# Block-sparse attention with a gated feed-forward layer: a second PSUM bank for the gate projections of two units, pad columns zeroed on VectorE, and a planner told longer load latencies

## The chip, the cores and the metric

The kernel runs on one core of a Trainium2 chip. A core has five engines that run side by side, each through its own list of instructions in order: TensorE (PE, matrix products into PSUM), VectorE (DVE), ScalarE (ACT), GpSimd (POOL) and SyncE (SP, which here only issues DMAs). They wait for each other through semaphores. The time is the device time of one execution in microseconds; lower is better.

## The reference, cut to what matters

First an attention over 4 batches, 8 heads, 768 positions and 64 columns per head, with a mask over blocks of 32 positions:

```python
scores = scale * np.matmul(q, k.transpose(0, 1, 3, 2))
mask = np.abs(blk_i - blk_j) <= window
mask = mask | (blk_i == 0) | (blk_j == 0) | (blk_i == n_blocks - 1) | (blk_j == n_blocks - 1)
for qb in range(n_blocks):
    for kb in sampled_blocks[qb]:
        mask[qb * block:(qb + 1) * block, kb * block:(kb + 1) * block] = True
scores = np.where(mask, scores, -1000000000.0)
scores = scores - np.max(scores, axis=-1, keepdims=True)
attn = np.exp(scores)
attn = attn / (np.sum(attn, axis=-1, keepdims=True) + 1e-09)
return np.matmul(attn, v).astype(np.float32)
```

Its output, laid out as 3072 tokens of 512 columns, is the input of the second part, with d_ff of 1536:

```python
rms = np.sqrt(np.mean(x * x, axis=-1, keepdims=True) + 1e-06)
xn = x / rms * rms_g
g = xn @ w_gate
silu = g * (1.0 / (1.0 + np.exp(-g)))
val = xn @ w_val
return (silu * val @ w_out).astype(np.float32)
```

## The kernel before, in words

All 768 x 768 scores are computed. The mask is part of the product: each row of q and k has 64 columns of data, and 24 more columns (one per key block) that add 0 or a large negative number, so 88 in all. These rows stand in two buffers `aug`, padded to 128 columns.

**Groups.** A group g is a pair of heads of one batch; there are 16, four per batch. For the four groups of batch 0, TensorE transposes the rows (`tp`, line 257) into PSUM, and an engine copies them into a slot of `XA` (`ev`, evacuation; `evx`, lines 260 to 262). For later groups the rows are loaded (`ld`), cast into `aug` (`fill`) and v into `vaug` (`pv`), and one transposing DMA, issued by SP, brings a whole group into `XA` (`turn`, line 243). It transposes all 128 columns, so the 40 pad columns must have been zeroed once (`zp`, line 247). `XA` has five slots. The q rows of columns 3 to 5 of batch 0 come by one load `q2`, and are cast by `fq` g 3.

**Units.** A unit u is a stretch of tokens of one batch: units 0, 1 and 2 are 128 tokens each, units 3 to 9 are 384 each (`UNITS`, lines 51 and 52). For each unit and each of the four pairs of heads come the scores (`qk`, line 275, in steps of 768 score columns that fill two PSUM banks), `exp` on ScalarE (line 290), the attention-value product `av` (line 304, bank 7, for units 0 to 2 also bank 6), and on VectorE the division `xo` (lines 315 and 316). When the four pairs are done come the square sums `sq`, the root `rsq` on GpSimd (line 333) and the scaling `xq` (line 340), then xn, the transposed input of the second part. For units below `NPET` (4 here) TensorE transposes xq (`tr`, line 351) and ScalarE or VectorE copies it (`cp`, line 359); for the others a transposing DMA does both (`xt`, line 366).

**Second part.** For each step f of a unit's d_ff: the gate projection `g` (line 378, bank 4), tanh of it on ScalarE (`th`, line 387), `uu` on VectorE (line 393), the value projection `v` (line 378, bank 5), and `hp` on VectorE (line 404). Last the output product `y` (line 417, bank 6), its copy `yo` and the store. `uu` gives the gate bank back and `hp` the value bank. Weights arrive in four chunks of w_gate and w_val (`wi` 0 to 3) and two of w_out, issued by GpSimd; chunks 2 and 3 are issued behind the roots of units 0 and 1. On SP a tiny DMA (`gate_sync`) waits for a chunk before the loads of groups 4 to 7.

**The order.** It is not written out by hand. A planner in the kernel (lines 689 to 753) holds a list of operations with the engines that may do each and a time for it, what it depends on, a priority, and what it takes and gives back (PSUM banks, buffers). It runs through a clock of its own, picks the operation that can start first and emits its instructions at once, on an engine of its choice where there are several. So a changed time, choice or bank can change the order on every engine from there on. On TensorE it also puts in dummy matmuls (`idle`) where it expects a gap within the first 24 us.

Behind a load, the planner counts 1.9 us (`LAT["DMA"]`) before the data is there, 8.0 for the loads of later batches:

```python
    end[o["key"]] = fin + (
        3.7 if o["key"] == ("q2",) else 8.0 if o["key"][0] == "ld" and o["key"][1] >= NP else 4.0 if o["key"][0] == "turn"
        else LAT[e])
```

Of the kernel before, what the change touches and what calls it, by code (L numbers as in the profile page):

```python
# [17 lines left out]
def kernel(  # L18
# [12 lines left out]
    nc = tc.nc  # L31
    SIMOUT = None
    P = 128
# [6 lines left out]
    NP = H // 2  # L40
# [3 lines left out]
    KQ = D + NB  # L44
    NSLOT, NAUG, NRAW, NOPEN = 5, 2, 3, 2
    AHEAD, HURRY, HURU = 0.8, ("av", "xo", "sq", "rsq", "xq", "tr", "cp"), 0
    NSTARV = 3
    AH = {"uu": 0.3, "hp": 0.3}
    WARM = (11, 10, 2)
    HD = NC * D // 2  # L50
# [3 lines left out]
    HG = [(b, c // 3) for b, c, n in UNITS]  # L54
# [16 lines left out]
    aug = [const.tile([P, 2, 2, NC, P], BF16, name=f"aug{i}") for i in range(NAUG)]  # L71
# [92 lines left out]
    for t in aug:  # L164
# [8 lines left out]
        op=ALU.is_equal)  # L173
# [24 lines left out]
    wg = const.tile([P, DM // P, DFF], BF16, name="wg")  # L198
# [45 lines left out]
            out=X[g % NSLOT].rearrange("p i e (c t) -> p (i e c) t", t=P),  # L244
            in_=aug[g % NAUG].rearrange("p i e c r -> p (i e c r)"))

    def zero_pad():
        for t in aug:
            nc.gpsimd.memset(t[:, :, :, :, KQ:P], 0.0)

    def tpx(g, i, es, lo, hi, bk):
        n = hi - lo
# [177 lines left out]
        dst = out[b * S:(b + 1) * S, :].rearrange("(p c) f -> p c f", c=NC)  # L430
        nc.sync.dma_start(out=dst[:, c0 + t, h * n:(h + 1) * n], in_=o)

    NPT, NXN, NHP, NPET = 3, 3, 2, 4
    pools = {n: [0.0] * c for n, c in (
        ("pt", NPT), ("hp", NHP), ("xo", 2), ("xq", 2), ("xn", NXN), ("raw", NRAW), ("va0", 1),
        ("va1", 1), ("th", 2), ("uu", 3))}
# [11 lines left out]
    def op(key, engs, deps, prio, fn, acq=(), rel=(), at=0.0):  # L448
        o = dict(key=key, engs=engs, deps=deps, prio=prio, fn=fn, acq=acq, rel=rel, at=at,
                 n=len(ops))  # L450
        ops.append(o)
        made[key] = o
# [56 lines left out]
    for g in range(NP):  # L509
        a_ = g % NAUG  # L510
        rr = [("raw", g)]
        if g:
            op(("fk", g), {"DVE": 0.57, "POOL": 0.84}, [("l", g, 0)], (-1, g, 0),
               lambda e, p, g=g: fillk(g, e), [(f"aK{a_}", g)], rr)
        for n_, (es, lo, hi) in enumerate(QP[g == 0]):
            dep = ("q2",) if lo == 3 else ("l", 0, 1, n_) if g == 0 else ("l", g, 1)
            pri = (-1, g, 1) if lo == 0 else (2.5, g, lo)
            fe = {"DVE": 0.09 + 0.085 * (hi - lo), "POOL": 0.1 + 0.13 * (hi - lo)}
            op(("fq", g, lo), {"ACT": 0.2} if g == 0 and lo == 0 else fe, [dep], pri,
               lambda e, p, a=(g, lo, hi): fillq(*a, e), [(f"a{'QR'[lo == 3]}{a_}", (g, lo == 3))],  # L520
               rr if lo < 3 else [("hp", ("q2",))])
        for i in range(2):
            for n_, (es, lo, hi) in enumerate((KP, QP)[i][g == 0]):
                m_ = len(es) * (hi - lo)
                if i == 0:
                    pri = (-1, g, 0.5 + 0.1 * n_ + (g == 0 and lo == 3))
                else:
                    pri = (-1, g, 1) if lo == 0 else (2.5, g, lo)
                res = f"aK{a_}" if i == 0 else f"a{'QR'[lo == 3]}{a_}"
                key = ("tp", g, i, es[0], lo)  # L530
                op(key, {"PE": m_ * 0.056}, [("fq", g, lo)] if i else [("fk", g)] if g else [],
                   pri, lambda e, p, a=(g, i, es, lo, hi): tpx(*a, p),
                   [(TP1[:1] if i and lo == 3 else TP1, key), (f"X{g}", g)],
                   [(res, g)] if i == 0 else [(res, (g, lo == 3))])
                de = {"DVE": 0.07 + m_ * P / 1560.0}
                ac = {"ACT": 0.15 + m_ * P / 1200.0}
                if g == 0 and i == 0:
                    de = (de, ac, {**de, **ac})[n_]
                elif i and lo == 3 or g == 0 and lo == 0:
                    de.update(ac)  # L540
                op(("ev",) + key[1:], de, [key], pri,
                   lambda e, p, a=(g, i, es, lo, hi): evx(*a, e), [], [(None, key)])
        op(("pv", g), {"DVE": 0.57, "POOL": 1.0}, [("l", g, 2)], (0, g, 2),
           lambda e, p, g=g: pad_v(g, e), [("va0", 0)], rr)
# [2 lines left out]
            pools[f"a{r_}{a_}"] = [0.0]  # L547
    held["aK0", 0] = "aK0"
    pools["aK0"] = []
    op(("zp",), {"POOL": 1.8}, [], (9,), lambda e, p: zero_pad(), at=24.0)  # L550
    for g in range(NP, B * NP):
        b, pr = divmod(g, NP)
        gate = {NP: 2, NP + 1: 3, NP + 2: 4, NP + 3: 5}.get(g)
        for i in range(3):
            def ld(e, p, g=g, i=i, gate=gate):
                if gate is not None and i == 0:
                    gate_sync(gate)
                load(g, i)
            op(("ld", g, i), {"DMA": 1.1}, [("w", gate)] if gate is not None and i == 0 else [],
               (1,), ld, [("raw", g)] if i == 0 else [])  # L560
            if i < 2:
                op(("fill", g, i), {"DVE": 0.57}, [("ld", g, i), ("zp",)] + [
                    ("tp", g_, i_, 0, 3 * i_) for g_ in (2, 3) for i_ in range(2)],
                   (4, g, i), lambda e, p, g=g, i=i: fill(g, i, e), [(f"aug{g % NAUG}", (g, False))])
            else:
                op(("pv", g), {"DVE": 0.57}, [("ld", g, 2), ("fill", g, 0), ("fill", g, 1)],
                   (4, g, 2), lambda e, p, g=g: pad_v(g, e), [(f"va{b % 2}", b)], [("raw", g)])
        op(("turn", g), {"DMA": 4.6}, [("fill", g, 0), ("fill", g, 1)], (-1, g),
           lambda e, p, g=g: turn(g), [(f"X{g % NSLOT}", g)], [(f"aug{g % NAUG}", (g, False))])
# [11 lines left out]
    for u, (b, c0, nt) in enumerate(UNITS):  # L581
        w, last = nt * P, c0 + nt == NC
        ng = NC // KT[nt]
        for pr in range(NP):
            g0 = b * NP + pr
            pk = pr // 2 if nt == 1 else pr
            for g in range(ng):
# [10 lines left out]
               lambda e, p, a=(u, pr): av(*a, p), [([(7,)] + [(6,)] * (u < 3), ("o", u, pr)), ("xo", u)],  # L598
               ([("pt", (u, pk))] if nt > 1 or pr % 2 else []) + ([(f"va{b % 2}", b)] if last and pr == NP - 1 else []))
            op(("xo", u, pr), {"DVE": 0.4 + w / 960.0}, [("av", u, pr)], (0, u, pr),  # L600
               lambda e, p, a=(u, pr): xo(*a), [], [(None, ("o", u, pr))])
# [18 lines left out]
        for f in range(NF // fg):  # L620
            n_ = fg * w
            op(("g", u, f), {"PE": fg * NP * mm(w)}, [("cp", u), ("w", w_of[f])], (4, u, f, 1),
               lambda e, p, a=(u, f): proj(*a, wg, "gp", p), [([(4,)], ("g", u, f)), ("hp", HG[u])])
            op(("th", u, f), {"ACT": 0.12 + n_ / 1200.0}, [("g", u, f)], (2, u, f),
               lambda e, p, a=(u, f): th(*a), [("th", (u, f))])
            op(("uu", u, f), {"DVE": 0.155 + n_ / 960.0}, [("th", u, f)], (2, u, f),
               lambda e, p, a=(u, f): uu(*a), [("uu", (u, f))],
               [(None, ("g", u, f)), ("th", (u, f))])
            op(("v", u, f), {"PE": fg * NP * mm(w)}, [("g", u, f)], (4, u, f, 0),
               lambda e, p, a=(u, f): proj(*a, wv, "vp", p), [([(5,)], ("v", u, f))],  # L630
               [("xn", u)] if f == NF // fg - 1 else [])
            op(("hp", u, f), {"DVE": 0.155 + n_ / 960.0}, [("uu", u, f), ("v", u, f)], (3, u, f),
               lambda e, p, a=(u, f): hp(*a), [],
               [(None, ("v", u, f)), ("uu", (u, f))])
# [54 lines left out]
    while ready:  # L689
# [27 lines left out]
        for names, key, nme in got:  # L717
# [9 lines left out]
        fin = t1 + o["engs"][e]  # L727
        free[e] = fin
        end[o["key"]] = fin + (
            3.7 if o["key"] == ("q2",) else 8.0 if o["key"][0] == "ld" and o["key"][1] >= NP else 4.0 if o["key"][0] == "turn"  # L730
            else LAT[e])
        if o["key"][0] in ("qk", "tr"):
            nqk -= 1
# [52 lines left out]
```

The softmax here doesn't subtract the row's maximum and nothing guards it: scores larger than these inputs give would overflow.

## Time and profile before

| | before |
|---|---|
| median of 7 runs (lowest to highest) | 312.06 us (311.75 to 315.37) |
| the profiled execution's own time | 312.06 us |
| its span, first to last instruction | 310.3 us |
| busy: TensorE, VectorE, ScalarE, GpSimd | 302.5, 191.4, 207.1, 24.3 us |
| granted TensorE clock | 1.000 |
| DMA: bytes, mean rate over the span | 42.42 MB, 137 GB/s |

Times are microseconds from the span's start. Matmuls overlap, so a group's duration is a little longer than the distance to the next group's start, and a short gap is seen in the starts more surely than in the row of waits. L and a number is a line of the kernel; the copies of many operations share line 113, and are told apart by their tiles.

### The profile page before, as it was taken

How to read it: one execution, taken by the hardware profiler on the slowest of the kernel's cores; microseconds unless marked ns; L12 is line 12 of the kernel's file. 1: busy time of each engine (PE TensorE's matmuls, PEld its weight loads, DVE VectorE, ACT ScalarE, POOL GpSimd, SP SyncE). 2: the span in 40 equal slices, each digit the busy share in tenths (PEclk: the TensorE clock that was granted, in tenths of full speed). 3: DMA queues.
4: the chain of work that ended last, by engine and by line, in shares of the span. 5: the costliest groups of instructions: out<-in, count | busy, mean ns of one | idle time of the engine just before them, and what ended most of it. 6: DMA issues, size and time to landing. Idle time of an engine off the chain costs nothing.

```text
span 310.3 us, 7395 instructions
## 1 busy us (share of the span) xinstructions
PE 302.5 (97%) x3063; PEld 200.7 (65%) x3063; DVE 191.4 (62%) x423; ACT 207.1 (67%) x325; POOL 24.3 (8%) x42
## 2 busy tenths in 40 slices
PE   8899999999999999999999999999999999999995
PEld 7898888766666656666666666666666545556543
DVE  5779655785668878766654844674489607727500
ACT  5988988688877877878777787878743133323221
POOL 3457200010000001001000100010001000000000
PEclk9999999999999999999999999999999999999999
DMA  6999999999999899931894030011000041010022
GB/s 210 315 233 195 195 268 221 215 307 282 228 306 196 227 214 323 235 122 36 159 159 75 34 87 2 34 38 49 2 34 3 17 127 45 0 70 0 0 105 101
DMA packets 70661, 42.42 MB, mean 137 GB/s; under 512 B 48356, under 2 KB 67556, under 8 KB 70628
## 3 DMA queue, kind: packets, MB, share of 16 engines
q1 hardware_dynamic: 64800, 37.23, 48.8%
q0 software_dynamic: 5792, 4.72, 9.7%
q8 instruction: 24, 0.39, 0.5%
q14 instruction: 9, 0.07, 0.1%
q10 hardware_dynamic: 36, 0.00, 0.0%
HBM read 28.57 MB, written 6.29 MB: 112 GB/s over the span
## 4 chain that ended last, share of the span: by engine, by line
PE 91%; DMA 3%; ACT 3%; DVE 2%; issue 1%; ACTq 0%; DVEq 0%; SPq 0%
PE PS L378 40%; PE PS L417 20%; PE PS L275 18%; PE PS L304 11%; ACT pt L290 2%; DMA qkv<-in_q_dram 2%; DMA xn<-xq 1%; PE PS L129 1%; PE PS L257 1%; DVE XA L113 1%; PE PS L351 0%; ACT th L387 0%; DVE uu L393 0%; DVE xo L316 0%; ACT XA L109 0%
## 5 line engine op out<-in xcount | busy, mean ns | idle before, releaser
L290 ACT ACTIVATE pt<-PS 128x768 bf16<-128x768 f32 x192 | 145.4, 812 | 35.2 <-PE PS L275 33.8
L393 DVE SCALAR_TENSOR_TENSOR uu<-th,PS 128x384 bf16<-128x384 bf16 x96 | 53.2, 554 | 62.3 <-ACT th L387 60.3
L275 PE MATMUL PS<-XA 88*128 88x384 bf16 (+1 forms) x480 | 81.4, 294 | 0.9 <-ACT pt L290 0.8
L378 PE MATMUL PS<-xn,wg 128*128 128x384 bf16 (+1 forms) x480 | 75.4, 294 | 1.1 <-DMA xn<-xq 0.7
L378 PE MATMUL PS<-xn,wv 128*128 128x384 bf16 (+1 forms) x480 | 75.5, 293 | 0.0
L417 PE MATMUL PS<-wo,hp 128*128 128x512 bf16 (+1 forms) x300 | 70.3, 370 | 0.0
L387 ACT ACTIVATE th<-PS 128x384 bf16<-128x384 f32 x96 | 47.4, 493 | 33.6 <-PE PS L378 31.2
L404 DVE TENSOR_TENSOR hp<-uu,PS 128x384 bf16<-128x384 bf16 x96 | 51.4, 551 | 15.0 <-PE PS L378 14.1
L378 PEld LDWEIGHTS <-wg 128*128 128x128 bf16 x480 | 41.6, 97 | 24.8 <-issue 1.6
L378 PEld LDWEIGHTS <-wv 128*128 128x128 bf16 x480 | 41.5, 97 | 23.3 <-issue 0.2
L275 PEld LDWEIGHTS <-XA 88*128 88x128 bf16 x480 | 39.6, 98 | 21.8 <-issue 1.8
L417 PEld LDWEIGHTS <-hp 128*128 128x128 bf16 x300 | 29.0, 98 | 26.9
L304 PEld LDWEIGHTS <-pt 128*128 128x128 bf16 x1152 | 41.2, 97 | 6.0 <-issue 0.7
L304 PE MATMUL PS<-vaug,pt 128*128 128x65 bf16 x1152 | 42.8, 193 | 0.6 <-DVE xo L316 0.6
L427 ACT ACTIVATE yo<-PS 128x512 f32<-128x512 f32 (+1 forms) x23 | 13.3, 579 | 28.0 <-PE PS L417 27.1
L333 POOL TENSOR_TENSOR rs<-ms,nhalf 128x3 f32<-128x3 f32 (+1 forms) x10 | 7.9, 787 | 200.3 <-DVE ms L326 200.3
L316 DVE TENSOR_TENSOR xo<-PS,rz 128x384 f32<-128x384 f32 (+1 forms) x40 | 19.1, 478 | 1.4
L340 DVE SCALAR_TENSOR_TENSOR xq<-xo,rs,gB 128x512 bf16<-128x512 f32 x24 | 17.5, 755 | 0.2 <-POOL rs L333 0.2
L326 DVE CUSTOM_DVE_ANT_0 sc<-xo 128x512 bf16<-128x512 f32 x24 | 16.5, 687 | 0.3
L113 DVE CAST aug<-qkv 128x768 bf16<-128x768 f32 (+2 forms) x30 | 15.2, 524 | 1.7 <-DMA qkv<-in_k_dram 1.2
L315 DVE RECIPROCAL rz<-PS 128x6 f32<-128x6 f32 (+1 forms) x40 | 7.4, 184 | 14.4 <-PE PS L304 14.3
L113 DVE CAST vaug<-qkv 128x768 bf16<-128x768 f32 x14 | 8.0, 574 | 1.5 <-DMA qkv<-in_v_dram 1.3
(54 smaller groups left out, 70.4 us busy)
## 6 DMA issues: line engine op xcount, KB each, us to landing
qkv<-in_v_dram SPq DMA_DIRECT2D x16, 384.0 KB, 5.7
out_dram<-yo SPq DMA_DIRECT2D x23, 256.0 KB, 2.0
qkv<-in_k_dram SPq DMA_DIRECT2D x15, 384.0 KB, 4.2
qkv<-in_q_dram SPq DMA_DIRECT2D x12, 384.0 KB, 4.8
wg<-in_moe_w_gate_dram POOLq DMA_DIRECT2D x4, 384.0 KB, 8.0
wv<-in_moe_w_val_dram POOLq DMA_DIRECT2D x4, 384.0 KB, 9.0
wo<-in_moe_w_out_dram POOLq DMA_DIRECT2D x2, 768.0 KB, 15.7
q<-in_q_dram SPq DMA_DIRECT2D x1, 768.0 KB
```

Source lines behind the costliest of these rows:

```text
L113: nc.vector.tensor_copy(out=out, in_=in_)
L275: nc.tensor.matmul(out=s_[:, e, j * w:(j + 1) * w], lhsT=x[0:KQ, 0, e, jt * P:(jt + 1) * P], rhs=x[0:KQ, 1, e, c0 * P:c0 * P + w], start=T ...
L290: nc.scalar.activation(out=pts[u, pr][:, g * kt:(g + 1) * kt].rearrange("p j e w -> p e j w"), in_=s_[:, :, 0:kt * w].rearrange("p e (j w) ...
L304: nc.tensor.matmul(out=o_[:, t, e, :], lhsT=pt[:, jt, e, t * P:(t + 1) * P], rhs=va[:, (2 * pr + e) * NC + jt, 0:D + 1], start=(jt == 0), ...
L316: nc.vector.tensor_tensor(out=xos[u][:, :, 2 * pr:2 * pr + 2, :], in0=o_[:, :, :, 0:D], in1=rz.unsqueeze(3).to_broadcast([P, nt, 2, D]), o ...
L326: nc.vector.tensor_tensor_reduce(out=sc, in0=x, in1=x, scale=1.0 / DM, scalar=1e-6, op0=ALU.mult, op1=ALU.add, accum_out=mss[u][:, t:t + 1])
L340: nc.vector.scalar_tensor_tensor(out=xqs[u][:, t, :], in0=xos[u][:, t].rearrange("p h d -> p (h d)"), scalar=mss[u][:, t:t + 1], in1=gB, o ...
L378: nc.tensor.matmul(out=p_[:, j, :].rearrange("p (t w) -> p t w", w=P), lhsT=w_[:, c, f_ * P:(f_ + 1) * P], rhs=xns[u][:, :, c, :], start=( ...
L387: nc.scalar.activation(out=t_, in_=tiles["gp", u, f], func=AF.Tanh, scale=0.5)
L393: nc.vector.scalar_tensor_tensor(out=t_, in0=tiles.pop(("th", u, f)), scalar=1.0, in1=tiles.pop(("gp", u, f)), op0=ALU.add, op1=ALU.mult)
L404: nc.vector.tensor_tensor(out=hps[u][:, f * fg:(f + 1) * fg, :], in0=tiles.pop(("uu", u, f)), in1=tiles.pop(("vp", u, f)), op=ALU.mult)
L417: nc.tensor.matmul(out=tiles["yp", u, t, h], lhsT=hps[u][:, f, t * P:(t + 1) * P], rhs=wo[:, f, x], start=(f == 0), stop=(f == NF - 1))
```

## The change

1. The pad columns are zeroed on VectorE, in two operations, one for each `aug` buffer, from 32.0 us of the planner's clock on; before, GpSimd did both in one, from 24.0 on. The fills of later groups depend on both.
2. `NPET` is 3: unit 3's xn comes by a transposing DMA (`xt`), as for the units after it.
3. The evacuation of the late query columns (`ev` with i of 1 and lo of 3) may no longer go to ScalarE.
4. The gate projections of units 3 and 4 may take bank 6 as well as bank 4.
5. For loads of batch 0 of groups 2 and 3 (and no others) the planner counts 2.6 us, not 1.9, before their data is there.

```diff
-    NSTARV = 3
+    NSTARV, ZPAT = 3, 32.0
...
-    def zero_pad():
-        for t in aug:
-            nc.gpsimd.memset(t[:, :, :, :, KQ:P], 0.0)
+    def zero_pad(i):
+        nc.vector.memset(aug[i][:, :, :, :, KQ:P], 0.0)
...
-    NPT, NXN, NHP, NPET = 3, 3, 2, 4
+    NPT, NXN, NHP, NPET = 3, 3, 2, 3
...
-                elif i and lo == 3 or g == 0 and lo == 0:
+                elif g == 0 and lo == 0:
                     de.update(ac)
...
-    op(("zp",), {"POOL": 1.8}, [], (9,), lambda e, p: zero_pad(), at=24.0)
+    for i in range(2):
+        op(("zp", i), {"DVE": 0.4}, [], (9,), lambda e, p, i=i: zero_pad(i), at=ZPAT)
...
-                op(("fill", g, i), {"DVE": 0.57}, [("ld", g, i), ("zp",)] + [
+                op(("fill", g, i), {"DVE": 0.57}, [("ld", g, i), ("zp", 0), ("zp", 1)] + [
...
-               lambda e, p, a=(u, f): proj(*a, wg, "gp", p), [([(4,)], ("g", u, f)), ("hp", HG[u])])
+               lambda e, p, a=(u, f): proj(*a, wg, "gp", p), [([(4,)] + [(6,)] * (2 < u < 5), ("g", u, f)), ("hp", HG[u])])
...
-            3.7 if o["key"] == ("q2",) else 8.0 if o["key"][0] == "ld" and o["key"][1] >= NP else 4.0 if o["key"][0] == "turn"
+            3.7 if o["key"] == ("q2",) else 2.6 if o["key"][0] == "l" and o["key"][1] > 1 else 8.0 if o["key"][0] == "ld" and o["key"][1] >= NP else 4.0 if o["key"][0] == "turn"
```

## The prediction

> **What bounds the kernel now.** I read the busy times and the slices first, then what TensorE waits for, then its instructions in order of time where it is not covered, then the other engines at those places.
>
> Of the page (busy us, share of the span, instructions; and tenths in 40 slices):
>
> ```profile
> PE 302.5 (97%) x3063; PEld 200.7 (65%) x3063; DVE 191.4 (62%) x423; ACT 207.1 (67%) x325; POOL 24.3 (8%) x42
> PE   8899999999999999999999999999999999999995
> PEclk9999999999999999999999999999999999999999
> DMA  6999999999999899931894030011000041010022
> ```
>
> TensorE works through the whole span and the other engines are at two thirds. So the time is TensorE's work plus the few gaps in it, and only a gap or a matmul that goes away shortens it. Of what TensorE waits for:
>
> ```profile
> PE PS L129 <- DVE zt L116: 1.1, 1, 1.1
> PE PS L275 <- ACT pt L290: 0.8, 4, 0.2
> PE PS L378 <- DMA xn<-xq: 0.7, 1, 0.7
> PE PS L304 <- DVE xo L316: 0.6, 1, 0.6
> PE PS L257 <- DVE XA L113: 0.5, 1, 0.5
> PE PS L378 <- DVE uu L393: 0.4, 2, 0.2
> ```
>
> These are small, and all lie before 110 us. The row shows a gap only past the modelled end of the last matmul, so I took the gaps from the starts instead: a group of 12 gate matmuls takes 0.67, 4 wide ones 0.65, 6 narrow score matmuls or transposes 0.34, 2 wide ones 0.33, 12 attention-value matmuls 0.38 and 36 of them 1.15. What a start is later than that is a gap. From the first score matmul (6.87) on, they add to 5.5 us, plus 16 dummy matmuls of 0.056 (0.9), 15 of them after 6.87. The dearest places, in TensorE's order of time (start, us, idle before):
>
> ```profile
> 26.24 0.50 PE L275 MATMUL PS<-XA 88*128 88x128 bf16 x6
> 27.32 0.94 PE L304 MATMUL PS<-vaug,pt 128*128 128x65 bf16 x24 [0.58 <-DVE xo L316]
> ...
> 67.54 0.83 PE L351 MATMUL PS<-ident,xq 128*128 128x128 bf16 x12
> 68.24 0.48 PE L275 MATMUL PS<-XA 88*128 88x384 bf16 x2
> ...
> 108.36 0.48 PE L275 MATMUL PS<-XA 88*128 88x384 bf16 x2
> 109.53 0.81 PE L378 MATMUL PS<-xn,wg 128*128 128x384 bf16 x4 [0.69 <-DMA xn<-xq]
> ```
>
> 26.24 + 0.33 to 27.32 is a gap of 0.75; 108.36 + 0.33 to 109.53 one of 0.84; the 12 transposes hold TensorE for 68.24 - 67.54 = 0.70. VectorE and GpSimd at the first of these:
>
> ```profile
> 24.29 2.58 DVE L113 CAST aug<-q 128x384 bf16<-128x384 f32 x1
> 26.79 0.15 DVE L315 RECIPROCAL rz<-PS 128x2 f32<-128x2 f32 x1
> ```
> ```profile
> 24.16 0.75 POOL L209 DMA_DIRECT2D wv<-in_moe_w_val_dram  x1
> 24.89 1.76 POOL L249 MEMSET aug<- 128x960 bf16 x2
> ```
>
> The same form of cast takes 0.35 elsewhere. This one ends 0.2 after GpSimd's second pad memset (24.89 + 1.76), and the reciprocals and xo behind it, which free PSUM for attention-value, come 2.2 late.
>
> **The change, part by part.** I compare the two built orders of instructions and price them with the rows above.
>
> *Unit 3's xn by DMA* (NPET 3). Gone are 12 transposes (0.70 of TensorE) and a ScalarE copy (1.44). Added is one transposing DMA behind unit 3's last xq. Unit 4's in the trace: xq ends 105.13, issue 105.17 (SP held 1.70), xn there at 109.53, so 4.4. In the new order, count from the last attention-value group of unit 3. Its xo ends at 2.05 (1.15, hand-over 0.2 as from a value group at 105.17 + 0.65 to its hp at 106.02, then 0.70). VectorE then has uu, hp, three square sums (0.7 each) and two more uu/hp pairs, the last hp behind the value projection that ends at 8.4; it ends at 9.1; three xq of 0.70 end at 11.2; xn is there at 15.6. TensorE meanwhile has 15.4 of work (36 attention-value, eight output groups, six 128-wide projections, 12 score groups, 36 more). Gap 0.2; I take 0.3. SP is a queue: ahead of this DMA stands group 5's transposing load (SP held 4.83 before, 7.83 at most), issued at about 0.5, then an output store and five loads of 0.5 and a gate of 0.6: free at about 9.5, or 12 with the longest hold, which would add 0.8. With 0.8 more for a slower flight the upper end is 1.9; the lower 0. Behind this DMA stand stores, loads and group 6's transposing load at about 14.9, landing in 7.0 (median; 10.0 at most), by 25 at the latest, needed at 25.2.
>
> *Gate projections of units 3 and 4 in bank 4 or 6.* In the new order 16 wide gate groups have no wait of their own, 3 before: a gate group no longer stands behind the uu of the one before it. The gap this saves is 103.17 + 0.33 to 103.87, 0.37. What it moves matters more: output groups of unit 3 no longer sit between its projections but after them, just ahead of unit 4's first gate group. From unit 4's last attention-value start to that gate group there is 14.5 of work; VectorE's last xq ends at 10.6 by the same walk (hp 3.1, square sum, uu, hp at 5.1, square sum, uu, square sum at 7.0, xo, hp at 8.5, three xq); xn is there at 15.0: gap 0.5, for 0.84 + 0.37 before and two of 0.09: -0.9. A store that holds bank 6 a little long, or loads of group 10 that land after VectorE wants them, give part back: I take -0.6, ends -1.2 and +0.8.
>
> *Zeroing on VectorE.* 1.76 of GpSimd goes, and with it the block above. Two memsets come at about 35 us, between xo and hp. They write 480 words of 4 bytes; nearest rows: 64 words 0.11, 144 elements 0.18, so [...]0.53 each; as 960 elements 1.0 at most. VectorE idles 0.35 to 1.2 before its hp there; without that cover each would hold one value bank for 0.5. Taken as 0.
>
> *Evacuations of the late query columns on VectorE alone, and 2.6 us for late loads.* ScalarE loses three copies of 0.80, VectorE gains three of 0.55. With the new latencies the planner also puts group 2's keys on GpSimd (0.82), swaps two other casts, and runs all 24 narrow exps on ScalarE before the first xn copy. What bounds this stretch is ScalarE's exps, 0.71 apart in a run. Work of TensorE from 6.87 to the first gate group: 144 narrow score matmuls, 4 wide ones, 72 + 4 transposes, ten attention-value groups: 8.16 + 0.65 + 4.30 + 3.82 = 16.93. In the trace that much work is done at 28.03, so 28.03 - 6.87 - 16.93 = 4.2 is lost. New: exps start at 7.57 and without a gap 24 end at 24.6. Walking the order with these rows: six exps end at 11.9. VectorE now has the first xo (to 10.9) ahead of pair 1's query columns (11.4); TensorE runs a value group, dummies and transposes to 11.8 and the score group to 12.15, so the exp starts at 12.33: gap 0.45. Ten exps follow to 19.43. Pair 3's transposes stand behind an evacuation, their copy behind an xo, until 19.32; score group to 19.73, exp at 19.9: gap 0.47. Four exps to 22.75. Meanwhile TensorE stands at 20.4 behind the cast of the q load, for which GpSimd waited until 20.28: done at 20.65 to 21.1; then transposes, scores, value group, transposes, scores (1.74): exp at 22.8 to 23.2. Four more. So 24 exps end at 26.0; xn copy, hand-over and gate group: +0.83, 26.8; lost 3.0; gain 1.2. Ends: no gap at all, 25.4 (gain 2.6); the trace's three ScalarE gaps again (0.36 + 0.46 + 0.45) and 1.0 at the q load, 27.7 (gain 0.3). Between 29 and 40 us the trace has gaps of 0.27, 0.32 and 0.16, two of them behind ScalarE's copies that are gone: -0.35, ends -0.75 and +0.3.
>
> *Weights and loads.* The third weight chunk follows the first unit's root on GpSimd, which by the walk ends at 24.0 to 24.4 (22.96 before), so about 1 us later; the gate DMA on SP behind it, and group 4's loads, shift by as much: v then lands at about 47.4, and VectorE stands before its cast for up to 1.4, ahead of a uu for which a gate group waits at 48.9. Covered mostly; +0.2, ends 0 and 1.5.
>
> **Rules of the Trainium skill.** "SBUF — State Buffer", section Who interferes with whom: VectorE and GpSimd share one port pair, taken for a whole instruction, and the other blocks fully; casts can take it. The 2.58 cast is that row. But the rule also speaks against this change: more of VectorE's casts now run beside GpSimd's, above all at the q load, where both cast at once. By the rule VectorE's waits all of GpSimd's 0.48; the row for an overlap is xq at 22.99, 0.98 for 0.74, so 0.24. With the rule in full the opening gains 1.0, with the row 1.2; I keep the row. "TensorE: Matmul & The Clock Gate", Part 1: about 3.4 us of idling halve the clock. Five of the dummy matmuls go; if one such window were lost, half of 3.4, 1.7, would be added. The granted clock is full in every slice and the longest gap after 6.87 is 0.84: nothing taken.
>
> **The sum.** -0.70 (transposes) - 1.2 (opening) - 0.35 (to 40 us) + 0.3 (unit 3's xn) - 0.6 (unit 4) + 0.2 (loads) = -2.35. The profiled execution took 312.06 over a span of 310.3, and the median of the seven runs is 312.06 too: **309.7**, span 308.0. After 110 us both orders do the same work without a gap, and the last 3.7 us (last store) stay.
>
> **Rivals.** *More* (307.5): the opening's gaps close, 25.4, and both xn waits vanish: -0.70 - 2.6 - 1.2 = -4.5. For it: ScalarE has slack after; against: three places in the order where TensorE, first in first out, stands behind VectorE. *It re-forms* (311.6): the q load lands later or VectorE, with 1.65 more of evacuations, sets the opening; only the transposes and little else remain. For it: DMA engines are full from 5 to 110 us. *The second bank does nothing* is part of this: gaps behind uu were only 0.37. *Slower* (314): unit 3's xn flies in the full stretch. The gain without it is 2.65, so slower by 1.56 needs a gap of 4.2, that is xn 8.4 after xq instead of 4.4. Against: six such DMAs took 3.6 to 4.4; for it: the transposing loads of twice the size took up to 10.0 and SP can be held 7.8.
>
> **How the numbers follow.** Under 0.5% (1.56 us) a measurement of this kernel tells nothing. Forecast 55% (its own range 308.2 to 310.5), more 8%, re-forms 22%, slower 15%: faster 63%, same 22%, slower 15%. To leave out no more than 2 in 10, the range goes from 307.8 to 313.2.
>
> **What would show it.** Right: no 2.6 us cast near 24 us; the first gate group at about 26.8; 12 transposes fewer; seven transposing xn DMAs; gaps of 0.2 to 0.5 before the first gate groups of units 3 and 4; nothing after 110 us. Wrong: a gate group of unit 3 that waits over 2 us for xn, ScalarE gaps of 0.5 and more between exps before 26 us, or scores waiting for transposing loads.

## The result, and the profile after

The changed kernel took 311.32 us (median of 25 executions, 309.6 to 316.68) against 312.16 for the kernel before (62 executions, 311.26 to 315.37): a ratio of 0.9968, with a 95% interval of 0.9949 to 0.9987. That is 0.3% faster where 0.8% was forecast, and less than the 0.5% taken as the least that can be told from no change. The profiled execution took 314.09 us over a span of 312.4, so it is one of the longer ones; why it is longer is the main thing to learn here. The ratios given here leave out executions over 1.5% above a kernel's fastest (five of 25 here, eight of 22 in experiment 1), so a ratio can differ from that of the two medians.

The page of the changed kernel (busy time; then forty slices of 7.8 us):

```profile
PE 303.1 (97%) x3046; PEld 200.1 (64%) x3046; DVE 192.1 (62%) x426; ACT 204.6 (66%) x322; POOL 23.9 (8%) x41
...
PE   8999999987999999999999999999999999999995
...
PEclk9999999997999999999999999999999999999999
DMA  7999999999799999950857030012000050020022
```

TensorE has 17 matmuls fewer: 12 transposes and five dummies. Its line has an 8 and a 7 at 62 to 78 us that the page before did not have, and in the second of these slices the granted clock shows a 7 too; the DMA engines are full (9) in the first. Of what TensorE waits for (us in total, times, longest), where xn had cost 0.7 before:

```profile
PE PS L377 <- DMA xn<-xq: 3.4, 2, 3.0
```

TensorE's timeline (start, duration, engine, line, output<-input, shape, count):

```profile
26.83 0.83 PE L377 MATMUL PS<-xn,wg 128*128 128x128 bf16 x12
...
68.68 0.49 PE L274 MATMUL PS<-XA 88*128 88x384 bf16 x2
72.20 1.46 PE L377 MATMUL PS<-xn,wg 128*128 128x384 bf16 x4 [3.04 <-DMA xn<-xq]
73.46 0.85 PE L274 MATMUL PS<-XA 88*128 88x384 bf16 x2
74.10 1.49 PE L377 MATMUL PS<-xn,wv 128*128 128x384 bf16 x4
...
111.16 0.48 PE L274 MATMUL PS<-XA 88*128 88x384 bf16 x2
112.06 0.81 PE L377 MATMUL PS<-xn,wg 128*128 128x384 bf16 x4 [0.41 <-DMA xn<-xq]
```

The first gate group starts at 26.83, where 26.8 was forecast. The first gate group of unit 3 waits until 72.20; by the starts (68.68 + 0.33 of work) TensorE stood 3.19 us. Then four 384-wide products take 1.46 us and not 0.81. Ahead of unit 4's first gate group (112.06) the gap is 0.57. Some stretches of this execution (stretch, length, busy PE, PEld, DVE, ACT, POOL, granted clock, DMA share, GB/s):

```profile
64.00:65.00 1.00, 0.94 (x27) 0.82 (x26) 0.82 (x2) 1.00 (x3) 0.00 (x0) 1.00 0.92 273
65.00:66.00 1.00, 1.00 (x21) 0.74 (x18) 0.43 (x2) 0.61 (x2) 0.00 (x0) 1.00 1.04 304
...
68.75:72.16 3.41, 0.42 (x3) 0.03 (x1) 0.00 (x0) 1.10 (x2) 0.00 (x0) 1.00 0.69 158
72.16:75.57 3.41, 3.37 (x14) 1.68 (x15) 0.56 (x1) 1.30 (x2) 0.00 (x0) 0.50 1.07 382
...
311.09:312.40 1.31, 0.00 (x0) 0.00 (x0) 0.00 (x0) 0.00 (x0) 0.00 (x0) 0.50 0.00 0
```

TensorE ran at half its clock from 72.16 on, for 3.41 us, right behind the wait, and again at the very end, where it had nothing left to do. The gaps between the starts of its groups (each group at its full-clock cost) give 0.61 + 0.31 + 0.63 + 0.10 = 1.65 us for that. The wait and the half clock cost 4.8 us together in this execution.

Why was xn late? SP's timeline:

```profile
62.06 0.40 SPq L80 DMA_DIRECT2D qkv<-in_k_dram  x1
62.51 0.47 SPq L80 DMA_DIRECT2D qkv<-in_q_dram  x1
63.02 0.47 SPq L80 DMA_DIRECT2D qkv<-in_v_dram  x1
64.42 3.41 SPq L365 DMA_TRANSPOSE xn<-xq  x1
```

The last xq ended at 64.34, which is 11.2 us after the start of the last attention-value group (53.17), as forecast, and the issue at 64.42 was prompt. But it held SP for 3.41 us (unit 4's before: 1.70), and xn landed 7.7 us after the issue and not 4.4. The three loads of group 7 had left SP 0.9 us earlier, and the first two stretches above show the DMA engines full (shares of 0.92 and 1.04) while the transpose queued.

The rest went close to the forecast. ScalarE's exps in the opening have their gaps where the walk had put them, 0.45 and 0.35 us (forecast 0.45 and 0.47), and the first 24 end at 25.87 (forecast 26.0). VectorE's timeline has the two memsets at 0.46 each (forecast 0.53) and the q cast beside GpSimd's at 0.58 in place of 0.35 alone (+0.23; the row had said 0.24, the rule of the port pair 0.48). The cast of 2.58 us is gone.

```profile
12.38 7.23 ACT L289 ACTIVATE pt<-PS 128x768 bf16<-128x768 f32 x10 [0.45 <-PE PS L274]
19.96 5.91 ACT L289 ACTIVATE pt<-PS 128x768 bf16<-128x768 f32 x8 [0.35 <-PE PS L274]
```

```profile
19.96 0.58 DVE L113 CAST aug<-q 128x384 bf16<-128x384 f32 x1
...
34.66 0.46 DVE L248 MEMSET aug<- 128x480 uint32 x1
```

### The profile page after: what moved, and what is told of

Read it like the earlier page. It is cut to its first block, busy times and chain, and to the rows that moved or that the text cites. A ratio compares the mean times of both kernels' runs of the same rounds, so it can differ in the third digit from the quotient of the medians.

```text
span 312.4 us, 7348 instructions
## 1 busy us (share of the span) xinstructions
PE 303.1 (97%) x3046; PEld 200.1 (64%) x3046; DVE 192.1 (62%) x426; ACT 204.6 (66%) x322; POOL 23.9 (8%) x41
## 4 chain that ended last, share of the span: by engine, by line
PE 90%; DMA 4%; ACT 2%; DVE 1%; issue 1%; POOL 0%; ACTq 0%
PE PS L377 41%; PE PS L416 18%; PE PS L274 18%; PE PS L303 11%; DMA xn<-xq 4%; ACT pt L289 2%; PE PS L256 1%; PE PS L129 1%; DVE xq L339 1%; PE PS L350 0%; PE PS L154 0%; DVE xo L315 0%; POOL rs L332 0%; ACT yo L426 0%; DVE rz L314 0%
## 5 line engine op out<-in xcount | busy, mean ns | idle before, releaser
L274 PE MATMUL PS<-XA 88*128 88x384 bf16 (+1 forms) x480 | 82.4, 294 | 0.5 <-ACT pt L289 0.4
L403 DVE TENSOR_TENSOR hp<-uu,PS 128x384 bf16<-128x384 bf16 x96 | 51.4, 551 | 16.3 <-PE PS L377 15.8
L426 ACT ACTIVATE yo<-PS 128x512 f32<-128x512 f32 (+1 forms) x24 | 14.0, 582 | 29.6 <-PE PS L416 29.3
L325 DVE CUSTOM_DVE_ANT_0 sc<-xo 128x512 bf16<-128x512 f32 x24 | 16.8, 699 | 0.4
L113 DVE COPY XA<-PS 88x768 bf16<-88x768 bf16 (+2 forms) x16 | 8.4, 529 | 3.6 <-PE PS L256 3.5
```

What stands on the lines that cost most here:

```text
L113: nc.vector.tensor_copy(out=out, in_=in_)
L274: nc.tensor.matmul(out=s_[:, e, j * w:(j + 1) * w], lhsT=x[0:KQ, 0, e, jt * P:(jt + 1) * P], rhs=x[0:KQ, 1, e, c0 * P:c0 * P + w], start=T ...
L325: nc.vector.tensor_tensor_reduce(out=sc, in0=x, in1=x, scale=1.0 / DM, scalar=1e-6, op0=ALU.mult, op1=ALU.add, accum_out=mss[u][:, t:t + 1])
L403: nc.vector.tensor_tensor(out=hps[u][:, f * fg:(f + 1) * fg, :], in0=tiles.pop(("uu", u, f)), in1=tiles.pop(("vp", u, f)), op=ALU.mult)
```

## The experiments

*Theory A*, as the profile above suggests it: the opening gives its gain. What was lost was lost at unit 3's wait for xn, because its DMA flies nearly twice as long behind loads that were issued just ahead, and part of the executions pay half a clock window on top. *Theory B*: something else in the new order costs the time. "Start gap" below is the distance from one group of TensorE to the next less the group's cost at full clock. "Planned work" is what the order on record puts on TensorE between a unit's last attention-value group and its first gate group: 13.8 us for unit 3 and 15.5 for unit 4 in the kernel before, 15.4 and 14.5 in the changed one. Each median stands beside that of the kernel before on the same chip.

### 1. Unit 3's transposes back on TensorE

```diff
-    NPT, NXN, NHP, NPET = 3, 3, 2, 3
+    NPT, NXN, NHP, NPET = 3, 3, 2, 4
```

> The changed kernel with unit 3's xn made by TensorE and a ScalarE copy again (NPET 4); all other parts of the change stay. Theory A (the transposing DMA of unit 3 costs 3.2 us of waiting, and the half clock behind it 1.65 more in the executions that show it): no gap over 0.5 us before unit 3's first gate group, the granted clock full, 0.70 of transposes back; against the profiled execution of the changed kernel (span 312.4) 312.4 - 3.2 - 1.65 + 0.7 = 308.2, time about 310.0, ratio to the kernel before about 0.993. Theory B (the wait merely shows where another shortage ends, for instance of weights or of group loads): the gap moves to another place within the next 10 us, time 311 to 312, ratio 0.997 or more.

Measured: 315.27 against 312.31, ratio 1.0011 (0.9978 to 1.0044). Of 22 executions 15 took over 313 us, all with a mean clock under 0.997; the other seven have a median of 312.0. Unit 3 waits no more, and the same loss has moved to unit 4. SP's and TensorE's timelines:

```profile
98.93 0.47 SPq L80 DMA_DIRECT2D qkv<-in_v_dram  x1
100.30 2.88 SPq L365 DMA_TRANSPOSE xn<-xq  x1
```

```profile
104.25 0.49 PE L274 MATMUL PS<-XA 88*128 88x384 bf16 x2
108.37 0.81 PE L377 MATMUL PS<-xn,wg 128*128 128x384 bf16 x4 [3.62 <-DMA xn<-xq]
```

Group 12's loads left SP at 99.40, 0.9 us ahead of the transpose; xn landed 8.1 us after its issue, the start gap was 3.79, and a half clock followed that cost some 1.6 us. Neither theory had put the loss here. So the loss is not tied to unit 3: unit 4's xn DMA, right behind loads, shows it too.

### 2. Dummy matmuls in unit 3's wait

```diff
+        if (kind, u, f) == ("gp", 3, 0):
+            idle(50, bk[0])
```

> The changed kernel with 50 dummy matmuls (2.8 us of TensorE) put straight ahead of unit 3's first gate group, where TensorE waits 3.2 us for xn; nothing else differs. Theory A (TensorE's idling of 3.2 us lets the clock fall to half for about 3 us, in some executions and not in others): the wait stays as long as it was, the granted clock stays 1.00 in every execution, the slow ones go (no time above 312.5), median about 309.9. Theory B (the lower clock has another cause, for instance the load of the chip): executions with a granted clock of 0.988 to 0.995 stay about 9 in 25, the median 311.3 or, with the dummies in the way, more.

Measured: 311.47 against 312.31, ratio 0.9963 (0.9941 to 0.9986), 17 executions from 310.8 to 312.8. The clock stayed at 1.00 from 60 to 116 us, and nothing above 313 us is left, where the changed kernel had 9 of 26 executions there: the half clock made those. But the median did not fall to 309.9. The dummies ran from 68.42 to 71.21, and xn had landed at 63.83 + 5.2 = 69.0 in this execution, so they cost about 2.2 us that nothing needed. SP's and TensorE's timelines:

```profile
61.45 0.47 SPq L80 DMA_DIRECT2D qkv<-in_v_dram  x1
63.83 2.41 SPq L365 DMA_TRANSPOSE xn<-xq  x1
```

```profile
68.42 2.96 PE L129 MATMUL PS<-zt 128*128 128x128 bf16 x50
```

SP's order is that of the changed kernel to the instruction, and so is all that stands ahead of the dummies. Yet the loads had left SP 1.9 us ahead of the transpose here, and not 0.9 (the transposing load before them held SP for 4.58 us, there for 5.57), and without the dummies TensorE would have waited 0.6 us and not 3.19. So the wait of one and the same order differs much from one execution to the next.

### 3. A planner told 6.0 us for unit 3's transpose

```diff
-            3.7 if o["key"] == ("q2",) else 2.6 if ...
+            6.0 if o["key"] == ("cp", 3) else 3.7 if o["key"] == ("q2",) else 2.6 if ...
```

> The changed kernel, but the planner counts 6.0 us, not 1.9, behind the issue of unit 3's transposing DMA; it then puts 18.2 us of TensorE's work between unit 3's last attention-value group and its first gate group, 15.4 before. Theory A (only the order is short of work there): the flight stays at 7 to 8, the gap falls from 3.2 to about 0.4, the clock stays full, span 312.4 - 2.8 - 1.65 = 307.9, time 309.7, ratio 0.992. Theory B (the work that is taken from behind is missed there): a new gap of 1 us or more before 110 us, time 310.5 or more.

Measured: 310.55 against 312.31, ratio 0.9915 (0.9879 to 0.9952). The flight was 5.5 us, with the loads 2.1 us ahead; the planned work ahead of unit 3's gate groups is now 18.2 us, and they do not wait for xn. That is theory A's direction, but not its figures: it had kept the flight at 7 to 8 us and put the time at 309.7, and 310.55 is a time that theory B had claimed. No new gap of 1 us shows in the profile, so B's mechanism is not seen either.

### 4. Group 7's loads behind unit 3's transpose

```diff
-            op(("ld", g, i), {"DMA": 1.1}, [("w", gate)] if gate is not None and i == 0 else [],
+            op(("ld", g, i), {"DMA": 1.1}, ([("w", gate)] if gate is not None and i == 0 else []) + [("cp", 3)] * (g == 7),
```

> The changed kernel with the three loads of group 7 (1.15 MB) held back until unit 3's transposing DMA has been issued, where they were issued 1 to 2 us ahead of it. Theory A (the transposing DMA took 7.7 us from issue to landing, not 4.4, because it stands behind these loads on the same DMA engines): it lands in 4 to 5.5, the gap falls to 0 to 1 us, the clock stays full, time about 309.5. Theory B (the flight is long whatever is ahead of it, because transposing loads and weights fill the engines until 120 us anyway): 7 us or more, the gap stays near 3, the time stays at 311. If the held loads come too late, scores of group 7 wait at about 85 us.

Measured: 310.72 against 312.31, ratio 0.9918 (0.9883 to 0.9954). The planned work ahead of the wait is unchanged (15.4 us). Up to unit 3's gate groups only the loads moved, and the flight fell from 7.7 to at most 4.6 us (the gate group finds xn there). Theory A had that, but a time of 309.5; the profile has three new gaps of 0.38 behind ScalarE's exps at 106 to 107.5 us. SP's timeline, TensorE's, and the stretches in which the transpose was issued (63 to 65 us; the columns as above):

```profile
59.64 0.49 SPq L80 DMA_DIRECT2D qkv<-in_v_dram  x1
64.07 1.42 SPq L365 DMA_TRANSPOSE xn<-xq  x1
```

```profile
68.34 0.49 PE L274 MATMUL PS<-XA 88*128 88x384 bf16 x2
68.67 0.81 PE L377 MATMUL PS<-xn,wg 128*128 128x384 bf16 x4
```

```profile
63.00:64.00 1.00, 0.95 (x9) 0.48 (x7) 1.00 (x3) 1.00 (x3) 0.00 (x0) 1.00 0.03 11
64.00:65.00 1.00, 0.99 (x31) 1.00 (x32) 0.48 (x2) 1.00 (x2) 0.00 (x0) 1.00 0.07 16
```

The DMA share at the issue is 0.03 to 0.07 here, against 0.92 to 1.04 in the changed kernel. SP is held 1.42 us and not 3.41.

### 5. The opening and the zeroing alone

The changed kernel with edit 2 (`NPET`) and edit 4 (the second bank) undone:

```diff
-    NPT, NXN, NHP, NPET = 3, 3, 2, 3
+    NPT, NXN, NHP, NPET = 3, 3, 2, 4
...
-               lambda e, p, a=(u, f): proj(*a, wg, "gp", p), [([(4,)] + [(6,)] * (2 < u < 5), ("g", u, f)), ("hp", HG[u])])
+               lambda e, p, a=(u, f): proj(*a, wg, "gp", p), [([(4,)], ("g", u, f)), ("hp", HG[u])])
```

> The changed kernel with unit 3's transposes back on TensorE and the gate projections of units 3 and 4 in bank 4 alone: what is left of the change is the opening (casts, planner's latencies) and the zeroing by VectorE. Planned TensorE work between unit 4's last attention product and its first gate group is 16.8 us, more than before (15.5). Theory A (the opening gives its gain, and what was lost was lost at waits for xn): 310.0 to 310.6 against 312.3 before, clock 1.00 in all windows from 60 to 116 us, no run above 313. Theory B (the opening gives little; the two kernels with a longer way for xn were lucky in their schedule): 311.5 to 312.3.

Measured: 310.08 against 312.03, ratio 0.9938 (0.9916 to 0.9960), six executions from 309.75 to 310.71. As theory A had it. The first gate group starts at 26.91, and the gap of 0.84 us ahead of unit 4's gate group is down to 0.24, with planned work of 16.8 us ahead of it.

### 6. Unit 3's xn by DMA alone

The kernel before with `NPET` 3, nothing else:

```diff
-    NPT, NXN, NHP, NPET = 3, 3, 2, 4
+    NPT, NXN, NHP, NPET = 3, 3, 2, 3
```

> The kernel before with unit 3's transposes by DMA and nothing else of the change. Planned TensorE work between unit 3's last attention product and its first gate group is 13.8 us, against 15.4 in the changed kernel. Theory A (xn flies some 7.7 us behind the loads of group 7, so the wait is that of the changed kernel and 1.6 us more, and TensorE's clock halves after it in most executions): wait of 4.7 us, 312.3 - 0.7 + 4.7 + 1.65 = 318.0; accepted from 315.5 up. Theory B (the flight of 4.4 us that the prediction took; the 7.7 was one execution's): wait of 1.4 us, 312.3 - 0.7 + 1.4 = 313.0.

Measured: 316.24 against 312.03, ratio 1.0122 (1.0080 to 1.0163). Edit 2 by itself is a loss of 1.2%. SP's and TensorE's timelines:

```profile
63.68 0.47 SPq L80 DMA_DIRECT2D qkv<-in_v_dram  x1
64.25 0.41 SPq L80 DMA_DIRECT2D qkv<-in_k_dram  x1
66.04 5.74 SPq L366 DMA_TRANSPOSE xn<-xq  x1
```

```profile
69.76 0.81 PE L417 MATMUL PS<-wo,hp 128*128 128x512 bf16 x3
74.78 1.44 PE L378 MATMUL PS<-xn,wg 128*128 128x384 bf16 x4 [4.21 <-DMA xn<-xq]
```

xn landed 8.7 us after the issue, the start gap was 4.37 us, and the half clock shows again in the 1.44 us of the gate group. Theory A had said 4.7 for the wait and 318.0 in all, and took 315.5 and more as its own; the flight of 4.4 us would have given 313.0.

### 7. The second bank alone

```diff
-               lambda e, p, a=(u, f): proj(*a, wg, "gp", p), [([(4,)], ("g", u, f)), ("hp", HG[u])])
+               lambda e, p, a=(u, f): proj(*a, wg, "gp", p), [([(4,)] + [(6,)] * (2 < u < 5), ("g", u, f)), ("hp", HG[u])])
```

> The kernel before with bank 6 beside bank 4 for the gate projections of units 3 and 4 and nothing else of the change. Planned TensorE work between unit 4's last attention product and its first gate group falls from 15.5 to 14.5 us; ahead of unit 3's it stays at 13.8. Theory A (the second bank pulls gate groups forward, to where xn of unit 4 isn't there yet): the wait at about 109 us grows from 1.2 to 2.2 us, and the clock halves there in more executions than before: median 313.3 to 314.5. Theory B (the second bank does nothing that shows): 312.0 to 312.6.

Measured: 310.95 against 312.03, ratio 0.9960 (0.9943 to 0.9977). Both theories missed. Unit 4's gate group no longer waits at all:

```profile
98.19 0.47 SPq L80 DMA_DIRECT2D qkv<-in_v_dram  x1
104.67 1.45 SPq L366 DMA_TRANSPOSE xn<-xq  x1
```

```profile
108.42 0.48 PE L275 MATMUL PS<-XA 88*128 88x384 bf16 x2
108.74 0.81 PE L378 MATMUL PS<-xn,wg 128*128 128x384 bf16 x4
```

The planned work ahead of it is shorter (14.5 us) than before (15.5), but the loads left SP 6.0 us ahead and not 2.9, and xn was there at most 4.1 us after its issue. So the planned work alone decides nothing; how close the loads stand matters as much. And the two parts do not add: the opening and zeroing alone gain 1.95 us, the bank alone 1.08, and both together are experiment 1, whose median is 3.0 higher than before (by its ratio they gain nothing). With both, the planned work ahead of unit 4's gate groups is down to 13.5 us and group 12's loads stand 0.9 us ahead of the transpose.

### 8. The kernel before, with dummies ahead of unit 4

```diff
+        if (kind, u, f) == ("gp", 4, 0):
+            idle(30, bk[0])
```

> The kernel before with 30 dummy matmuls (1.7 us) ahead of the first gate group of unit 4, where TensorE waits for xn. Theory A (the times of the kernel before above 314 us, about one in five, are executions in which that wait is long enough for the clock to be halved after it): no run above 313.9, median 312.2 to 313.0, because the dummies fill a wait of about 1.2 us and add 0.5. Theory B (those times come from elsewhere, the opening for one): about one run in five stays above 314 us, and the median rises by the 0.5 that the dummies take.

Measured: 312.92 against 312.03, ratio 1.0051 (1.0026 to 1.0076), and three of 13 executions at 314.9 to 316.2. Theory B: the long executions of the kernel before do not come from that wait. The dummies took 1.67 us and filled a wait of about 0.8.

### 9. Experiment 1 with group 12's loads behind unit 4's transpose

```diff
-    NPT, NXN, NHP, NPET = 3, 3, 2, 3
+    NPT, NXN, NHP, NPET = 3, 3, 2, 4
...
-            op(("ld", g, i), {"DMA": 1.1}, [("w", gate)] if gate is not None and i == 0 else [],
+            op(("ld", g, i), {"DMA": 1.1}, ([("w", gate)] if gate is not None and i == 0 else []) + [("cp", 4)] * (g == 12),
```

> The changed kernel with unit 3's transposes on TensorE (the kernel that took 315.3 us), and the three loads of group 12 issued behind unit 4's DMA transpose in place of just ahead of it. TensorE's planned order is the same to the instruction. Theory A (a DMA transpose issued within some 1.5 us of three loads flies 7.7 to 8.7 us, and within 3 us or more 3.7 to 4.6): unit 4's transpose holds SP for some 1.5 us and not 2.9, xn lands 4.0 to 4.6 us after its issue, the wait falls from 3.6 to at most 0.5 us, the clock stays at 1.00 from 104 to 116 us: 309.7 to 310.5. Theory B (13.5 us of planned work ahead of unit 4's gate groups is simply too little, whatever the loads do): the wait stays at 2.5 us or more, 314 to 315.5.

Measured: 311.27 against 312.09, ratio 0.9972 (0.9959 to 0.9985), 22 executions from 310.43 to 312.39. TensorE's order is that of experiment 1 to the instruction, and the median is 4.0 us lower (by the ratios the gain is 0.4%; among executions at full clock the medians are 312.0 and 311.3). SP's and TensorE's timelines:

```profile
98.31 0.45 SPq L80 DMA_DIRECT2D qkv<-in_v_dram  x1
100.08 1.59 SPq L365 DMA_TRANSPOSE xn<-xq  x1
```

```profile
104.03 0.49 PE L274 MATMUL PS<-XA 88*128 88x384 bf16 x2
105.52 0.81 PE L377 MATMUL PS<-xn,wg 128*128 128x384 bf16 x4 [1.00 <-DMA xn<-xq]
```

The wait falls from 3.6 to 1.0 us, the clock stays full, and no execution is above 312.4. The forecast of 309.7 to 310.5 was missed by 0.8 us, since two loads of group 11 now stand 1.3 us ahead and the flight is 5.4 us, not 4.0 to 4.6.

### 10. A load put just ahead of a transpose that had none

Experiment 5's kernel, with one more line changed:

```diff
+            op(("ld", g, i), {"DMA": 1.1}, ([("w", gate)] if gate is not None and i == 0 else []) + [("xq", 4, 0)] * (g == 12),
```

> The kernel with the opening and the zeroing alone (310.1 us, no wait for xn), with the three loads of group 12 held until the first of unit 4's normalised tiles is there, so that they are issued just ahead of its DMA transpose, at about 102.7 to 104.2 us, and not 4.8 us before it. No order of instructions changes on any engine. Theory A (loads issued just ahead make the transpose fly 7.7 us and more): SP held 2.4 us or more, xn lands at about 113.4 instead of by 109.7, a wait of some 3.2 to 3.7 us, and in part of the executions the half clock behind it: 313 to 315.5. Theory B (the long flights of the other kernels had another cause): flight at most 4.5 us, 310.0 to 310.6.

Measured: 311.07 against 312.09, ratio 0.9958 (0.9940 to 0.9976), so 1.0 us more than experiment 5. The new dependency binds the planner's order, not the chip. Two of the three loads still left early; only v, which now stands behind a store on SP, was issued just ahead:

```profile
105.81 0.42 SPq L80 DMA_DIRECT2D qkv<-in_v_dram  x1
106.33 2.28 SPq L365 DMA_TRANSPOSE xn<-xq  x1
```

```profile
109.30 0.49 PE L274 MATMUL PS<-XA 88*128 88x384 bf16 x2
111.39 0.81 PE L377 MATMUL PS<-xn,wg 128*128 128x384 bf16 x4 [1.60 <-DMA xn<-xq]
```

The time lies between the two theories because the dose was a third of what was meant: one load just ahead gives 5.1 us of flight, and a start gap of 1.76 where experiment 5 had 0.2. The clock stayed full behind it.

### 11. Both transposes planned at 6.0 us

```diff
-            3.7 if o["key"] == ("q2",) else 2.6 if ...
+            6.0 if o["key"] in (("cp", 3), ("cp", 4)) else 3.7 if o["key"] == ("q2",) else 2.6 if ...
```

> The changed kernel with 6.0 us instead of the general latency in the planner for the transposes of units 3 and 4 both: planned work ahead of the first gate groups 18.2 and 19.5 us (15.4 and 14.5 in the changed kernel). Theory A (what the change lost was lost at waits for xn; the 12 transposes of unit 3 are worth their 0.7 us once nothing waits): no wait for xn, 308.9 to 309.7, below the 310.1 of the kernel with the opening and the zeroing alone. Theory B (TensorE has other work to lose by the later gate groups; taking the transposes from it brings nothing): 310.1 to 310.9.

Measured: 309.13 against 312.09, ratio 0.9904 (0.9877 to 0.9930), six executions from 308.78 to 309.44. This beats both kernels. TensorE's timeline around the two gate groups:

```profile
70.86 0.81 PE L274 MATMUL PS<-XA 88*128 88x384 bf16 x4
71.50 0.81 PE L377 MATMUL PS<-xn,wg 128*128 128x384 bf16 x4
...
111.55 0.81 PE L416 MATMUL PS<-wo,hp 128*128 128x512 bf16 x2
112.20 0.81 PE L377 MATMUL PS<-xn,wg 128*128 128x384 bf16 x4
```

Unit 3's xn still flew 6.1 us (loads 1.7 us ahead), but 18.2 us of planned work covered it.

### 12. The zeroing alone

The kernel before with edit 1 only:

```diff
-            nc.gpsimd.memset(t[:, :, :, :, KQ:P], 0.0)
+        nc.vector.memset(aug[i][:, :, :, :, KQ:P], 0.0)
...
-    op(("zp",), {"POOL": 1.8}, [], (9,), lambda e, p: zero_pad(), at=24.0)
+        op(("zp", i), {"DVE": 0.4}, [], (9,), lambda e, p, i=i: zero_pad(i), at=ZPAT)
```

> The kernel before with the pad columns zeroed by VectorE at about 32 us and nothing else of the change (casts and latencies of the opening as before, TensorE transposes for unit 3, one bank). Theory A (zeroing takes a stretch of GpSimd off the opening but the gain of the opening comes from the latencies and the evacuation, as the prediction had it with 1.2 us against 0.35): 311.4 to 312.1. Theory B (the zeroing brings most of the 1.95 us that opening and zeroing brought together): 310.1 to 310.9.

Measured: 311.23 against 312.09, ratio 0.9973 (0.9955 to 0.9992), just under the range of theory A and far above that of B. The cast of 2.58 us is gone (0.35 at 24.84), as the prediction had it, and so is the gap of 0.75 ahead of 27.32. The first gate group is later (26.12, before 25.57), behind a wait of 1.5 us at 15.4. But up to 24.9 us the order on every engine is that of the kernel before, so this wait, in which VectorE stood for a load of k, is one execution's and not the edit's. Unit 4's gate group starts without a gap at 109.92, its xn having landed 3.7 us after the issue with the loads 6.5 us ahead. The zeroing gains 0.86 us; that edits 3 and 5 bring the rest of experiment 5's 1.95 follows from the two medians, and the single profiles are too unlike to show where.

## Why the prediction was wrong, step by step

**What was right.** The opening: 16.93 us of work, done at 28.03 before, is done at 26.83, the forecast gain of 1.2. That it fits to the hundredth is chance: in the nine traces with the new opening the first gate group starts between 26.25 and 27.59. From there to 60 us the start gaps fall from 0.82 to 0.25 (forecast -0.35). Opening and zeroing alone gave 1.95 us, unit 4's gap included. Unit 4's gate group in the changed kernel: a gap of 0.57 behind the group at 111.16 (forecast 0.5), and the 0.37 behind `uu` is gone (-0.64 in all, forecast -0.6). The transposes: experiment 11 is 0.95 us under experiment 5, neither with a row for xn among its waits; 0.70 was counted (the two also differ by the second bank, so this agrees and does not prove). The weights and loads: no gap over 0.16 between 27 and 62 us, where +0.2 was put.

**The step that failed** is "Unit 4's in the trace: ... so 4.4", carried over to unit 3, and from it the gap of 0.3 with its upper end of 1.9. The prediction saw the five loads on SP ahead of this DMA and asked only when SP would be free. It did not ask what those loads still had to move. They had left SP 0.9 us before, while the DMA engines were full. The flight was 7.7 us, and the gap in the profile 3.19. The rest of the walk held: xq ended 11.2 us after the last attention-value group's start, as forecast, and TensorE was ready after 15.8 (forecast 15.4); xn came after 19.0 and not after 15.6.

The runs give the size of this term. Flight of an xn DMA from its issue, by how long before it the last load had left SP:

| loads just ahead | flight | SP held |
|---|---|---|
| three or more, 0.9 to 1.4 us ahead (changed kernel; 1; 6) | 7.7, 8.1, 8.7 | 3.41, 2.88, 5.74 |
| one, 0.1 us ahead (10) | 5.1 | 2.28 |
| two, 1.3 us ahead (9) | 5.4 | 1.59 |
| three, 1.7 to 2.1 us ahead (11; 2; 3) | 6.1, 5.2, 5.5 | 2.07, 2.41, 2.45 |
| none for 2.9 us or more (before; changed kernel, unit 4; 4; 12) | 4.4, 4.6, at most 4.6, 3.7 | 1.70, 1.51, 1.42, 1.42 |

These are DMAs that a first gate group depends on. In all 14 traces a flight, to the landing or to the gate group that waited for it, can be read for 57 xn DMAs. The 11 with a load out of SP in the 2.3 us before took 4.7 to 8.7 us. The other 46 took 3.6 to 5.1, but for one of 5.8 (unit 4's in experiment 6, loads 2.8 us ahead); so the time since the last load is a guide and no limit.

Experiments 4 and 9 moved the loads alone and brought the flight down; experiment 10 moved one load alone and brought it up. So that the loads cause the long flight is shown. How closely, the landings tell: the last load ahead of unit 3's transpose landed at 70.97 in the changed kernel and xn 1.19 us later; in experiments 2, 3 and 11 xn followed that load by 1.22, 1.21 and 1.20 us, though the flights were 5.2, 5.5 and 6.1. The way in which they do it is told by a page of the Trainium skill, "DMA: Bandwidth & Descriptors", section Queues, rings and completion order: SP has one ring on each DMA engine, and each engine takes the descriptors (the orders for single moves) of a ring in order. The transpose's then come up only behind those of the loads, and the full DMA shares at 64 to 66 us and the steady 1.2 us agree with it; no run here puts the transpose on another queue, which would separate a ring's order from mere sharing of a busy engine. Read that way, the prediction's own walk would have said: three loads, 0.9 us old, on full engines.

**The rival that came true in part** is *Slower*, which named this place, and needed a gap of 4.2, xn 8.4 after xq. The gap was 3.19, but the rival lacked a second cost. "Nothing taken" for the clock was right only as long as no gap exceeded 0.84. The half clock lasted 3.41 us and cost 1.65. The Trainium skill's "TensorE: Matmul & The Clock Gate", Part 1, gives a window of about 3.4 us and half rate after an idle one, from which one estimates a loss of 1.7. The same part says that the window runs free of the program, and the traces show it. In the changed kernel the stretch behind the wait begins at 72.16 and the one at the end at 311.09, which is 238.93 us or 70 windows of 3.413 apart; in experiments 1 and 6 the two are 204.80 and 242.35 us apart, 60 and 71 windows. So how much of a wait falls into one window is a matter of chance, which fits that a wait of this size halves the clock in some executions and not in others: of the changed kernel's 26 executions with a clock on record 17 had a mean of 0.997 or more and took 309.6 to 312.57 us, nine had 0.995 or less and took 313.18 to 316.68. If the window just ahead is the one that counts, it need not be idle throughout, as the page's "idle window" would have it: TensorE worked for 0.42 of the 3.41 us ahead of 72.16, and in experiment 1, where the half clock begins at 109.69, it had been at work again since 108.37. A wait of 1.76 us (experiment 10) did not halve the clock.

**The sum again, with what was measured:** -0.70 (transposes, as counted) - 1.2 - 0.57 (opening) - 0.64 (unit 4) + 3.19 (unit 3's xn) + 1.65 (half clock) = +1.73, so a span of 312.0 against 312.4 in the profile; of the 0.4 left, 0.23 is a gap at 65.34, behind an attention-value group, and the rest stays without a name. The executions without the half clock have their median at 311.0. That is 1.3 above the forecast, which leaves room for a mean wait of 1.6 where 0.3 was put. That the wait varies, experiment 2 shows (0.6 for the same order); how it is spread is not shown. Nor was the flight all of it: experiment 4 has about the assumed flight and no wait for unit 3, and took 310.72, 1.0 above the forecast, with new gaps behind the exps. With both waits covered (experiment 11) the kernel takes 309.13.

**What stays open.** The kernel before also has executions with a mean clock under 0.997 (17 of 137 beside the experiments, at 313.5 us and more). So have experiments 7, 8 and 12, which share its opening, 12 up to 24.9 us (8 of 57). In the seven experiments with the new opening and no wait over 1.8 us (2 to 5 and 9 to 11) there are none in 91. That points to the old opening; which of its gaps does it no profile caught. Three of the changed kernel's nine long executions have a mean clock of 0.988 or 0.989, as much as two lost windows would make; where the second lies no profile shows.

## What to carry to other kernels

The flight of a DMA is no constant of its shape: read what was issued on the same queue in the microseconds ahead of it, and take a row with the same neighbours. An edit that pulls compute forward toward a DMA's landing, or loads back toward its issue, can cost several times what it saves, and two edits that each gain can gain nothing together, or lose; so plan a transfer on the critical path with its latency under load, which here meant one number in the planner (6.0 us for two transposes) and some 2 us of gain (ratios of 0.9904 and 0.9968). One profile is one draw: the same order waited 3.19 us in one execution and would have waited 0.6 in another. Where TensorE may idle about 3 us, add the half clock behind it to the price.

## What had not been expected

- The same transposing DMA of 128 x 1536 flew 3.7 to 8.7 us, and held SP 1.42 to 5.74 us, mostly with the loads issued in the two microseconds ahead of it, and landed 1.2 us behind the last of them.
- An idle stretch of 3.19 us in TensorE was followed by 3.41 us at a granted clock of 0.50, worth 1.65 us, in a window that runs free of the program; 3.79 and 4.37 us of idling (experiments 1 and 6) did the same, 1.16 and 1.76 us (9 and 10) did not.
- Opening and zeroing alone -1.95 us, second bank alone -1.08 us, both together +3.0 in the median.
